# Second MLP's last tiles and first experts: splits of the experts' weights at fixed steps, each ordered behind routing and evictions; the seventh tile's logits later

## The chip, the core and the metric

The kernel runs on one core of a Trainium2 chip. Its time is the device time of one execution in microseconds (us): 430.04 us median of three runs (427.2 to 432.1). One further execution was profiled; it took 430.29 us, and the recorded span of its instructions is 428.2 us.

## The reference

Three layers follow each other; each needs the one before.

```python
attn = softmax(q @ k.T / 8 + decay bias, causal) @ v           # 2 batches x 8 heads, 576 positions, depth 64
x    = attn as 1152 tokens x 512
h    = x @ w_in;  x = (h * cos(h)) @ w_out                     # 512 -> 2048 -> 512, "the MLP"
logits = x @ w_gate;  expert = argmax(logits)                  # 8 experts, top 1
disp[expert, position of the token within the expert] = x      # capacity 288 per expert
y   = relu(disp[e] @ w1[e]) @ w2[e]                            # 512 -> 1024 -> 512, for each expert
out[token] = softmax weight * y[expert, position]
```

## The kernel before

Every float32 operand is held as two float16 parts (high and low), and each product is three float16 products.

**MLP, second product.** 1152 tokens are nine tiles of 128 (T = 0 to 8). `l2_wide` does tiles 0 to 4 side by side, `l2r` does tiles 5 to 8 one after the other, each in 8 steps of two of the 16 slices of the inner dimension: six matmuls a step (line 867). At a tile's end `l2_end` evicts the sum: for tiles 7 and 8 a float32 copy into `xq` (L856, ACT), and for all tiles the row's high part (L858, ACT) and low part (L859, DVE).

**Routing**, woven into the same steps by `l2r`: `route_a` turns the tile, by a DMA transpose on SP's queue for tiles 0 to 6 (L895), by TensorE and a copy on ACT for tiles 7 and 8 (L900, L902). `route_b`, RD = 2 steps later, makes the logits (L917, or L914 in float32), their maximum and the one-hot row on DVE (L927 to L931), the position within the expert by a matmul with a triangle (L936), the count `cnt` (L946), and a scatter of the row into `disp` in HBM (L947, POOL). After tiles 4 and 7 `partial` chooses, from the counts so far, which expert is worked on second and third; its number is loaded into a register of SP (L1170). Before tile 7's routing `hook` issues the DMA transposes `eX<-disp` of the first 144 rows of the first two experts (L1013) and their meta rows (L1020). After tile 8 `counts` orders the experts, SP loads seven numbers (L1210, L1211), issues `eX<-disp` for the rows of these two experts that came later (80 rows each in the shape that ran), and loads the shape number `fl` (L1342), on which every engine branches into its arm.

**Experts' weights.** An expert's w1 and w2 come as eight pieces of 128x1024 float32 (512 KB): SP loads a piece into a staging buffer `ws` (L969 for w1, L973 for w2; three buffers until the first experts, then four), `split` makes the high part on ACT (L658) and the low part on DVE (L659), and the buffer is free again. `e_weights` is a generator: each `next` first fills the free buffers, then splits one piece. The first expert's eight pieces are split beside `l2_wide`. The second's eight and four of the third's come from `ahead`, one per step from step 10 on wherever the expert's number is known; the third's last four follow after `counts`. The remaining 40 pieces are loaded and split in the arm.

**First experts**, `expert`: eight groups of 12 matmuls (L1044) give the hidden layer, each evicted by ACT (L1046) and DVE (L1047) into `eH`; then four groups of 24 matmuls d0 to d3 (L1066), each copied by ACT into `xq` (L1068); then eight transposes (L1073), and the result is scaled (L1052) and scattered into `out` (L1053). RF = 2 groups of the first expert run before tile 8's routing ends, and LA = 4 groups of the second before the first's d0.

**What sets the order.** A scheduler orders each engine's instructions at build time from the program's order and its own estimate; at run time every engine takes its instructions strictly in that order. `after(keys, ...)` adds an edge of order behind the last instruction stored under a key of `gate`; in the kernel before a split stands behind the last `ev` (eviction of an expert) and `cnt` (end of `counts`).

Of the kernel before, what the change touches and what calls it, by code (L numbers as in the profile page):

```python
# [15 lines left out]
ALU = mybir.AluOpType  # L16
# [9 lines left out]
W3P = 12  # L26
# [26 lines left out]
RP = 2  # L53
RD = 2
RF = 2
W2P = 24
# [21 lines left out]
def kernel(ctx, tc, q, k, v, s, w_in, w_out, wg, w1, w2, out, cap, wide):  # L78
# [773 lines left out]
    def l2_end(T, xp):  # L852
        r = work.tile([128, ROW], I32, tag="row", name="row", bufs=6)
        xf = xq[:, 0:DM] if T >= NDT else None
        if T >= NDT:
            nc.scalar.activation(xf, xp, AF.Copy, scale=2.0 ** -2)  # L856
        rh = r[:, 0:DM].bitcast(F16)
        nc.scalar.activation(rh[:, 0:DM], xp, AF.Copy, scale=2.0 ** -8)  # L858
        nc.vector.scalar_tensor_tensor(rh[:, DM:2 * DM], xp, 2.0 ** -8, rh[:, 0:DM], ALU.mult, ALU.subtract)  # L859
        nc.gpsimd.tensor_copy(r[:, DM + 1:ROW], tokid[:, T:T + 1])  # L860
        rows[T] = (r, xf)
# [29 lines left out]
    def route_a(T):  # L891
        r, xf = rows[T]
        if T < NDT:
            xr = work.tile([128, 2 * KD, 128], F16, tag="xr", name="xr", bufs=2)
            nc.sync.dma_start_transpose(out=xr, in_=r[:, 0:DM].bitcast(F16))  # L895
            rows[T] = (r, xr)
        else:
            tp = bank("pt")
            for kk in range(KD):
                nc.tensor.transpose(tp[:, kk * 128:(kk + 1) * 128], xf[:, kk * 128:(kk + 1) * 128], idf)  # L900
            xt = xq[:, DM:2 * DM].rearrange("p (k t) -> p k t", k=KD)
            nc.scalar.copy(xt.rearrange("p k t -> p (k t)"), tp)  # L902
            rows[T] = (r, xt)

    def route_b(T):
# [30 lines left out]
        nc.tensor.matmul(ppv, lhsT=tri, rhs=oh.to_broadcast([128, 2, E]), start=False, stop=True)  # L936
        nc.scalar.activation(ex, lp, AF.Exp, bias=m[:, 1:2], scale=LS, accum_out=m[:, 3:4])
        V.tensor_scalar(t1, ppv[:, 1, :], float(cap), float(NOTOK), ALU.is_ge, ALU.mult)
# [6 lines left out]
        V.tensor_scalar(r[:, DM:DM + 1].bitcast(F32), m[:, 3:4], 2.0 ** -17, None, ALU.mult)  # L945
        V.tensor_tensor(cnt[:, 0, :], cnt[:, 0, :], oh[:, 0, :], ALU.add)  # L946
        sc = nc.gpsimd.indirect_dma_start(  # L947
# [10 lines left out]

    def e_weights(plan, lo=0, hi=None):
        n = KD + KE // 2  # L960
# [17 lines left out]
        def fill(n):  # L978
            while todo and len(pend) < n and not (callable(todo[0][1]) and todo[0][1]() is None):
                ld(*todo.pop(0))  # L980

        fill(len(ws) - 1)
        yield
        for e, src, i in items:
# [5 lines left out]
            if i < KD:  # L990
                after("ev cnt", split, a[0][:, i, 0, :], a[0][:, i, 1, :], t, 64.0)
            else:
                j = (i - KD) * 2
                after("ev cnt", split, a[1][:, j:j + 2, 0, :], a[1][:, j:j + 2, 1, :], t.rearrange("p (a d) -> p a d", a=2), 64.0)
            yield
# [34 lines left out]
    def expert(e, ns, group, got=None):  # L1030
# [7 lines left out]
        for f in range(KE):  # L1038
# [7 lines left out]
            gate["ev"] = nc.scalar.activation(Hh[:, 0, f, :], hp[:, 0:ns], AF.Relu)  # L1046
            nc.vector.scalar_tensor_tensor(Hh[:, 1, f, :], hp[:, 0:ns], 0.0, Hh[:, 0, f, :], ALU.max, ALU.subtract)  # L1047
            yield
# [60 lines left out]
    def l2r(tiles, hook):  # L1109
# [13 lines left out]
        for T in tiles:  # L1123
            for j in range(KF // 2):
                next(gen)
                if mid and step - mid[0][1] >= RD:
                    finish()
# [29 lines left out]
    def partial():  # L1157
# [10 lines left out]
        V.tensor_copy(si, so[:, 0:1])  # L1168
        V.tensor_scalar(si, si, E - 1, E - 1, ALU.bitwise_and, ALU.bitwise_xor)
        P["o"].append(nc.values_load(si, engines=SP, min_val=0, max_val=E - 1))  # L1170
# [43 lines left out]
    def experts(plan, group):  # L1214
# [25 lines left out]

        gate.pop("ev", None)
        gate.pop("cnt", None)

# [53 lines left out]
    with ExitStack():  # L1297
        if True:
# [3 lines left out]
            items = KD + KE // 2  # L1302
            pre = e_weights([(i, i if i < NF else (lambda i=i: P["o"][i] if i < len(P["o"]) else None)) for i in range(NK)])
            run((l2_wide(range(WN), seq(wo, take(pre, items + 1)), L2F), KF + 1))
# [10 lines left out]
            def ahead(steps):  # L1315
                k = items
                for i in range(steps):
                    if i > KF // 2 + 1 and k < min(len(P["o"]) * items, 2 * items + KD):
                        next(pre)
                        k += 1  # L1320
                    yield
                while k < 2 * items:
                    next(pre)
                    k += 1

# [4 lines left out]
            phase, phase1 = (expert(h, HEAD, "out0", ex_.pop(h)) for h in range(NH))  # L1330
            for _ in range(RF):
                next(phase)
            next(tail)
            regs = counts()
            for _ in range(KE // 2):
                next(pre)
            order, first = registers(*regs)
            for h in range(NH):
                n = max(p[h] for p in PROFILES)
                e_rows(h, n, at(P["o"][h], first[h], n))  # L1340
            run((seq(take(phase, KE - RF), take(phase1, LA), phase, phase1), 2 * (KE + KD)), (take(pre, items), W3P))
            level = nc.values_load(regs[0], min_val=0, max_val=len(LIMITS))  # L1342
# [42 lines left out]
```

## Time and profile before

| | |
|---|---|
| median of three runs | 430.04 us |
| profiled execution | 430.29 us, span 428.2 us |
| TensorE (PE) | 395.1 us busy, 92% |
| VectorE (DVE) / ScalarE (ACT) / GpSimd (POOL) | 311.8 / 274.8 / 149.2 us busy |
| loads of the experts' weights | 64 of 512 KB, on SP's queue |

The second product of the MLP runs from about 194 to 293 us, the first two experts' 144 rows from 293 to 325 us, the arm from there to the end. A row of a timeline gives the start and the length of an instruction or a run of like ones; in brackets stands how long the engine was idle before it, and what ended that. SPq is SP's instruction queue: its rows give when a DMA was issued, not when it landed.

### The profile page before, as it was taken

Reading aid. Unit: us, or ns where it says so; the run is one execution under the profiler, and the core shown is the slowest. Engines: PE = TensorE matmul, PEld = TensorE weight load, DVE = VectorE, ACT = ScalarE, POOL = GpSimd, SP = SyncE. Lnnn points to the kernel's source line nnn. Section 1 sums busy time; section 2 is a strip of 40 time slices with the busy share of each in tenths; the row PEclk is TensorE's granted clock in tenths of the full one; section 3 lists DMA queues with packets and bytes.
Section 4 is the critical chain, followed back from the end, with each engine's and each line's share of the span. In section 5 each row is a group of like instructions: output and inputs, shape, how many; then the busy total and the mean of one; then the engine's idle time right before and its main releaser. Section 6 shows DMA issues by size and latency. Waiting matters only on the chain.

```text
span 428.2 us, 10640 instructions
## 1 busy us (share of the span) xinstructions
PE 395.1 (92%) x3928; PEld 281.6 (66%) x3928; DVE 311.8 (73%) x768; ACT 274.8 (64%) x630; POOL 149.2 (35%) x261
## 2 busy tenths in 40 slices
PE   2799999999999999999999999797998999999783
PEld 2588888886666666654444454354997999987552
DVE  7769999749999599989885664672842477877670
ACT  6679989986878677775234532533734477777560
POOL 7668887563554445455000032010011011122100
PEclk9989999999999999999999999899999999999998
DMA  7979795203369932323667456947759298998851
GB/s 166 210 173 190 165 203 151 72 2 100 98 188 328 369 124 92 88 70 98 183 204 230 116 128 206 280 110 222 252 148 216 61 314 264 308 330 265 264 209 30
DMA packets 90003, 77.38 MB, mean 181 GB/s; under 512 B 62768, under 2 KB 70960, under 8 KB 89942
## 3 DMA queue, kind: packets, MB, share of 16 engines
q1 hardware_dynamic: 86934, 71.62, 59.5%
q0 software_dynamic: 1952, 4.73, 3.2%
q8 instruction: 33, 0.54, 0.5%
q10 hardware_dynamic: 1056, 0.26, 0.3%
q14 instruction: 28, 0.23, 0.2%
HBM read 57.66 MB, written 12.28 MB: 163 GB/s over the span
## 4 chain that ended last, share of the span: by engine, by line
PE 32%; DMA 9%; DVE 7%; issue 5%; ACT 4%; SPq 2%; POOL 1%; POOLq 0%; ACTq 0%; DVEq 0%
DMA ws<-in_moe_w_dram 8%; PE ps_mm L867 7%; PE ps_sm L867 5%; PE ps_pt L1044 3%; PE ps_s L1066 3%; PE ps_mm L1044 2%; PE ps_s L867 2%; PE ps_pt L867 2%; PE ps_s L1044 2%; PE ps_pt L1066 2%; PE ps_mm L1066 2%; DVE gall L659 1%; ACT gall L658 1%; DVE y L818 1%; SPq L1013 1%
## 5 line engine op out<-in xcount | busy, mean ns | idle before, releaser
L812 PEld LDWEIGHTS <-win 128*128 128x128 f16 x576 | 56.3, 98 | 37.0
L867 PEld LDWEIGHTS <-gall 128*128 128x128 f16 x432 | 41.3, 98 | 49.3 <-issue 2.5
L867 PE MATMUL ps_mm<-wout,gall 128*128 128x512 f16 x240 | 57.9, 387 | 0.3 <-DVE n__2954 L826 0.3
L659 DVE SCALAR_TENSOR_TENSOR gall<-ws,gall 128x1024 f16<-128x1024 f32 x32 | 38.8, 1221 | 23.2 <-ACT gall L658 22.1
L1053 POOL DMA_INDIRECT out_dram<-gall,eM x15 | 18.8, 1252 | 98.4 <-ACT gall L1052 77.4
L658 ACT ACTIVATE gall<-ws 128x1024 f16<-128x1024 f32 x32 | 33.7, 1056 | 26.8 <-DMA ws<-in_moe_w_dram 26.8
L658 ACT ACTIVATE wout<-ws 128x512 f16<-128x512 f32 (+1 forms) x32 | 27.3, 860 | 23.7 <-DVE ws L681 18.5
L241 ACT ACTIVATE z<-z,st 128x256 f32<-128x256 f32 (+4 forms) x72 | 41.9, 586 | 0.7 <-DVE st L241 0.7
L947 POOL DMA_INDIRECT disp<-row,rsli x9 | 9.2, 1017 | 94.0 <-ACT rm L928 48.5
L241 DVE CUSTOM_DVE_ANT_0 z<-ps_s,zm 128x512 f32<-128x512 f32 (+3 forms) x72 | 34.5, 511 | 10.0 <-PE ps_s L244 8.8
L659 DVE SCALAR_TENSOR_TENSOR wout<-ws,wout 128x512 f16<-128x512 f32 (+1 forms) x32 | 30.4, 955 | 8.2 <-ACT wout L658 8.0
L812 PE MATMUL ps_s<-xT,win 128*128 128x384 f16 x192 | 34.2, 326 | 0.0
L812 PE MATMUL ps_pt<-xT,win 128*128 128x384 f16 x192 | 33.8, 326 | 0.0
L812 PE MATMUL ps_mm<-xT,win 128*128 128x384 f16 x192 | 33.8, 326 | 0.0
L247 PE MATMUL ps_pt<-idf,z 128*128 128x128 f32 x192 | 30.2, 282 | 1.3 <-DVE p L241 1.3
L1044 PEld LDWEIGHTS <-gall 128*128 128x128 f16 x480 | 27.0, 97 | 3.7 <-issue 1.9
L825 ACT ACTIVATE y<-y,quarter 128x384 f32<-128x384 f32 x48 | 29.2, 609 | 0.1
L241 ACT COPY p<-ps_pt 128x512 f32<-128x512 f32 (+2 forms) x48 | 25.2, 525 | 5.9 <-PE ps_pt L247 5.5
L659 DVE SCALAR_TENSOR_TENSOR win<-ws,win 128x1024 f16<-128x1024 f32 x16 | 19.4, 1225 | 11.7 <-ACT win L658 11.7
L247 PEld LDWEIGHTS ps_pt<-idf,z 128*128 128x128 f32 x192 | 23.1, 144 | 6.3 <-issue 1.5
L244 PE MATMUL ps_s<-kT,qT 128*128 128x384 f16 (+7 forms) x128 | 23.9, 307 | 1.1 <-DMA kT<-bt 0.6
L658 ACT ACTIVATE win<-ws 128x1024 f16<-128x1024 f32 x16 | 16.8, 1055 | 10.9 <-DMA ws<-in_moe_w_dram 10.9
(495 smaller groups left out, 891.9 us busy)
## 6 DMA issues: line engine op xcount, KB each, us to landing
ws<-in_moe_w_dram SPq DMA_DIRECT2D x64, 512.0 KB
ws<-in_moe_w_in_dram SPq DMA_DIRECT2D x16, 512.0 KB
ws<-in_moe_w_out_dram SPq DMA_DIRECT2D x16, 512.0 KB
disp<-zc SPq DMA_DIRECT2D x18, 257.0 KB
out_dram<-zc SPq DMA_DIRECT2D x9, 256.0 KB
qf<-in_q_dram SPq DMA_DIRECT2D x16, 128.0 KB
vf<-in_v_dram SPq DMA_DIRECT2D x16, 128.0 KB
kf<-in_k_dram SPq DMA_DIRECT2D x14, 128.0 KB
```

The costliest lines, as they stand in the source:

```text
L241: return pin(f(*a, **kw))
L244: return pin(nc.tensor.matmul(out_, **kw))
L247: return pin(nc.tensor.transpose(out_, in_, id_))
L658: nc.scalar.activation(hi, src, AF.Copy, scale=sc)
L659: (eng or nc.vector).scalar_tensor_tensor(lo, src, sc, hi, ALU.mult, ALU.subtract)
L812: nc.tensor.matmul(hp[:, 0:CH], lhsT=win[a][:, kk, fs], rhs=xT[:, x_, kk, xs], start=(n == 0), stop=(n == 3 * KD - 1))
L825: nc.scalar.activation(y, y, AF.Sin, scale=TWO_PI, bias=quarter)
L867: gate["pe"] = nc.tensor.matmul(xp, lhsT=G[c][:, a, f, ts], rhs=wout[w_][:, f, :], start=(f == 0 and n == 0), stop=(f == KF - 1 and n == 2))
L947: sc = nc.gpsimd.indirect_dma_start(out=disp, out_offset=bass.IndirectOffsetOnAxis(ap=sli.bitcast(U32), axis=0), in_=r, in_offset=None, bo ...
L1044: gate["pe"] = nc.tensor.matmul(hp[:, 0:ns], lhsT=a1[:, kk, a, fs], rhs=X[:, x_ * KD + kk, 0:ns], start=(n == 0), stop=(n == 3 * KD - 1))
L1053: sc = nc.gpsimd.indirect_dma_start(out=out, out_offset=bass.IndirectOffsetOnAxis(ap=M[:, b, 1:2].bitcast(U32), axis=0), in_=y, in_offset= ...
L1066: nc.tensor.matmul(yp[:, 0:ns], lhsT=a2[:, f, w_, d * 128:(d + 1) * 128], rhs=Hh[:, a, f, :], start=(n == 0), stop=(n == 3 * KE - 1))
```

## The change

The splits before the arm are made at fixed steps, two tables say where: `AHEAD` for the second expert's eight pieces (steps of tiles 5 to 8; step 16 is the first of tile 7), `HEADS` for the third's eight (groups of the first experts; negative ones are the two that run ahead, 0 is after `counts`). Every split now also stands behind the last eviction or routing instruction on its engine (`act`, `dve`). After each split the freed buffer's load is asked for at once (`ctl["fill"]`). The logits of tile 6, the seventh, come RL = 5 steps after its turn instead of 2.

```diff
+RL = 5
+AHEAD = (16, 17, 18, 20, 22, 24, 26, 28)
+HEADS = (-2, -1, 0, 0, 3, 5, 7, 9)
...
-        nc.scalar.activation(rh[:, 0:DM], xp, AF.Copy, scale=2.0 ** -8)
-        nc.vector.scalar_tensor_tensor(rh[:, DM:2 * DM], xp, 2.0 ** -8, rh[:, 0:DM], ALU.mult, ALU.subtract)
+        gate["act"] = nc.scalar.activation(rh[:, 0:DM], xp, AF.Copy, scale=2.0 ** -8)
+        gate["dve"] = nc.vector.scalar_tensor_tensor(rh[:, DM:2 * DM], xp, 2.0 ** -8, rh[:, 0:DM], ALU.mult, ALU.subtract)
...
-            nc.scalar.copy(xt.rearrange("p k t -> p (k t)"), tp)
+            gate["act"] = nc.scalar.copy(xt.rearrange("p k t -> p (k t)"), tp)
...
-        nc.scalar.activation(ex, lp, AF.Exp, bias=m[:, 1:2], scale=LS, accum_out=m[:, 3:4])
+        gate["act"] = nc.scalar.activation(ex, lp, AF.Exp, bias=m[:, 1:2], scale=LS, accum_out=m[:, 3:4])
...
-        V.tensor_tensor(cnt[:, 0, :], cnt[:, 0, :], oh[:, 0, :], ALU.add)
+        gate["dve"] = V.tensor_tensor(cnt[:, 0, :], cnt[:, 0, :], oh[:, 0, :], ALU.add)
...
+        if ctl is not None:
+            ctl["fill"] = lambda: fill(len(ws))
...
-                after("ev cnt", split, a[0][:, i, 0, :], a[0][:, i, 1, :], t, 64.0)
+                after("ev cnt act dve", split, a[0][:, i, 0, :], a[0][:, i, 1, :], t, 64.0)
...
-            nc.vector.scalar_tensor_tensor(Hh[:, 1, f, :], hp[:, 0:ns], 0.0, Hh[:, 0, f, :], ALU.max, ALU.subtract)
+            gate["dve"] = nc.vector.scalar_tensor_tensor(Hh[:, 1, f, :], hp[:, 0:ns], 0.0, Hh[:, 0, f, :], ALU.max, ALU.subtract)
...
-                if mid and step - mid[0][1] >= RD:
+                if mid and step - mid[0][1] >= (RL if mid[0][0] == NDT - 1 else RD):
...
             def ahead(steps):
-                k = items
                 for i in range(steps):
-                    if i > KF // 2 + 1 and k < min(len(P["o"]) * items, 2 * items + KD):
+                    if i == AHEAD[0] - 4:
+                        ctl["fill"]()
+                    for _ in range(AHEAD.count(i)):
                         next(pre)
-                        k += 1
+                        ctl["fill"]()
                     yield
-                while k < 2 * items:
-                    next(pre)
-                    k += 1
...
-            for _ in range(RF):
+            ctl["fill"]()
+
+            def pulls(i):
+                for _ in range(HEADS.count(i)):
+                    next(pre)
+                    ctl["fill"]()
+
+            for i in range(RF):
                 next(phase)
+                pulls(i - RF)
             next(tail)
             regs = counts()
-            for _ in range(KE // 2):
-                next(pre)
+            pulls(0)
             order, first = registers(*regs)
...
-            run((seq(take(phase, KE - RF), take(phase1, LA), phase, phase1), 2 * (KE + KD)), (take(pre, items), W3P))
+            for i, _ in enumerate(seq(take(phase, KE - RF), take(phase1, LA), phase, phase1)):
+                pulls(i + 1)
```

Lines of the changed kernel stand 3 to 13 further down: its L661 is L658 of the kernel before, L859, L861 and L905 are L856, L858 and L902, L1051 is L1046, L1073 is L1068, L1217 is L1211, L1018 is L1013, L976 is L973, L1355 is L1342. In the rows of the order `ws_90`, `ws_91` and `ws_92` are the three staging buffers, `ws_4090` and `ws_4079` the fourth one, `gall` is where the second and third experts' split weights go.

First place: ACT at the end of tile 8 (`xq<-ps_mm` is its float32 copy, `xq<-ps_pt` its turned copy for the logits). Before:

```order
L658 ACTIVATE gall<-ws_90 128x1024
L856 ACTIVATE xq<-ps_mm 128x512
L858 ACTIVATE row<-ps_mm 128x512
L658 ACTIVATE gall<-ws_91 128x1024
L902 COPY xq<-ps_pt 128x512
L658 ACTIVATE gall<-ws_92 128x1024
L1046 ACTIVATE eH<-ps_s 128x144
```

With the change:

```order
L661 ACTIVATE gall<-ws_92 128x2x512
L859 ACTIVATE xq<-ps_mm 128x512
L861 ACTIVATE row<-ps_mm 128x512
L905 COPY xq<-ps_pt 128x512
L1051 ACTIVATE eH<-ps_s 128x144
L661 ACTIVATE gall<-ws_90 128x1024
```

The third expert's first three splits stood ahead of or between tile 8's evictions; now its first stands behind them and behind the first eviction of an expert. On PE the logits of tile 6 move from behind 38 of the matmuls that follow tile 5's L936 to behind 49, and its L936 follows 5 matmuls later instead of 9.

Second place: ACT at the four copies of the first expert's d0 to d3. Before:

```order
L658 ACTIVATE gall<-ws_90 128x2x512
L1068 COPY xq<-ps_s 128x144
L1068 COPY xq<-ps_pt 128x144
L1068 COPY xq<-ps_mm 128x144
L1068 COPY xq<-ps_s 128x144
L1052 ACTIVATE gall<-ps_pt,eM_3443 72x512
```

With the change:

```order
L1073 COPY xq<-ps_s 128x144
L1073 COPY xq<-ps_pt 128x144
L661 ACTIVATE gall<-ws_92 128x2x512
L1073 COPY xq<-ps_mm 128x144
L661 ACTIVATE gall<-ws_4079 128x2x512
L1073 COPY xq<-ps_s 128x144
L1057 ACTIVATE gall<-ps_pt,eM_3443 72x512
```

The third expert's last two splits, all done before d0's copy until now, stand ahead of the copies of d2 and d3.

Third place: SP's queue between the last loads of the third expert and the branch. Before, the last two of these loads come first:

```order
L973 ISA
L973 DMA ws_4090<-in_moe_w_dram 128x2x512
L973 ISA
L973 DMA ws_90<-in_moe_w_dram 128x2x512
L1210 TENSOR_LOAD si
```

With the change:

```order
L1217 TENSOR_LOAD si
L1217 ISA x2
L1018 ISA
L1018 DMA_TRANSPOSE eX<-disp 128x8x80
L1018 ISA
L1018 DMA_TRANSPOSE eX<-disp 128x8x80
L976 ISA
L976 DMA ws_92<-in_moe_w_dram 128x2x512
L976 ISA
L976 DMA ws_4079<-in_moe_w_dram 128x2x512
L1355 TENSOR_LOAD fl
```

These two loads, which the two splits of the second place read, now stand behind the seven register loads and both `eX` transposes of the later rows.

## Rows read from the trace of the kernel before

**Rows 1.** Stretches: us, busy PE, PEld, DVE, ACT, POOL, PEclk, DMA share, GB/s.
```profile
274.00:278.00 4.00, 3.87 (x21) 1.61 (x22) 2.25 (x7) 2.61 (x6) 0.00 (x0) 0.57 0.96 294
296.00:298.00 2.00, 1.32 (x19) 1.31 (x20) 1.82 (x2) 2.00 (x5) 0.00 (x0) 1.00 0.85 314
380.00:400.00 20.00, 18.11 (x224) 14.39 (x222) 12.87 (x20) 13.62 (x28) 3.16 (x2) 1.00 0.87 294
```
**Rows 2.** The chain that ended last, 255 to 345 us: start, us, what.
```profile
262.47 4.16 DMA ws<-in_moe_w_dram
273.07 1.07 ACT gall L658
282.08 3.22 DMA disp<-row,rsli
```
**Rows 3.** The timeline of PE.
```profile
263.10 6.85 PE L867 MATMUL ps_mm<-wout,gall 128*128 128x512 f16 x31
274.13 0.46 PE L917 MATMUL ps_s<-wgs,xr 128*128 128x8 f16 x12 [2.62 <-ACT gall L658]
274.45 3.77 PE L867 MATMUL ps_mm<-wout,gall 128*128 128x512 f16 x9
296.68 0.65 PE L900 MATMUL ps_pt<-idf,xq 128*128 128x128 f32 x4 [2.95 <-ACT xq L856]
303.74 0.17 PE L1181 MATMUL ps_sm<-cnt,onesm 128*128 128x8 f16 x1
306.81 1.66 PE L1066 MATMUL ps_s<-eH,win 128*128 128x144 f16 x24
313.48 0.49 PE L1073 MATMUL ps_mm<-idf,xq 128*72 128x128 f32 x3
313.81 0.91 PE L1044 MATMUL ps_s<-eX,gall 128*128 128x144 f16 x12
```
**Rows 4.** The timeline of ACT.
```profile
267.61 0.58 ACT L858 ACTIVATE row<-ps_mm 128x512 f16<-128x512 f32 x1
295.09 1.06 ACT L658 ACTIVATE gall<-ws 128x1024 f16<-128x1024 f32 x1 [7.80 <-DMA ws<-in_moe_w_dram]
313.01 0.28 ACT L1068 COPY xq<-ps_s 128x144 f32<-128x144 f32 x1 [1.22 <-PE ps_s L1066]
345.86 1.06 ACT L658 ACTIVATE wout<-ws 128x1024 f16<-128x1024 f32 x1 [0.16 <-DMA ws<-in_moe_w_dram]
```
**Rows 5.** The timeline of DVE.
```profile
275.30 0.16 DVE L927 TENSOR_REDUCE rm<-ps_s 128x1 f32<-128x8 f32 x1
275.95 0.23 DVE L931 TENSOR_SCALAR roh<-rw,rm 128x8 f16<-128x8 f32 x1
304.67 0.16 DVE L1192 TENSOR_SCALAR si<-si 1x8 int32<-1x8 int32 x1
```
**Rows 6.** The timeline of SP's queue.
```profile
269.59 1.27 SPq L895 DMA_TRANSPOSE xr<-row  x1
291.45 6.31 SPq L969 DMA_DIRECT2D ws<-in_moe_w_dram  x4
310.64 2.77 SPq L1013 DMA_TRANSPOSE eX<-disp  x2
340.71 4.62 SPq L973 DMA_DIRECT2D ws<-in_moe_w_dram  x3
```
**Rows 7.** The timeline of POOL.
```profile
305.44 0.97 POOL L947 DMA_INDIRECT disp<-row,rsli  x1 [11.89 <-DVE ky L1198]
```
**Rows 8.** Two lines' instructions, 240 to 332 us: duration in ns, first and last start.
```profile
L1210 SPq TENSOR_LOAD <-si x5: 172/272/488, 304.9 to 307.2; - x5
L1211 SPq TENSOR_LOAD <-si x2: 275/276/276, 308.0 to 308.9; - x2
```

More of the change, by code (lines that the diff above doesn't have):

```diff
@@ L957, with e_weights @@
     wb = []
-    def e_weights(plan, lo=0, hi=None):
+    def e_weights(plan, lo=0, hi=None, ctl=None):
         n = KD + KE // 2
@@ L990, in e_weights @@
             if i < KD:
-                after("ev cnt", split, a[0][:, i, 0, :], a[0][:, i, 1, :], t, 64.0)
+                after("ev cnt act dve", split, a[0][:, i, 0, :], a[0][:, i, 1, :], t, 64.0)
             else:
                 j = (i - KD) * 2
-                after("ev cnt", split, a[1][:, j:j + 2, 0, :], a[1][:, j:j + 2, 1, :], t.rearrange("p (a d) -> p a d", a=2), 64.0)
+                after("ev cnt act dve", split, a[1][:, j:j + 2, 0, :], a[1][:, j:j + 2, 1, :], t.rearrange("p (a d) -> p a d", a=2), 64.0)
             yield
@@ L1168, in partial @@
         V.tensor_copy(si, so[:, 0:1])
-        V.tensor_scalar(si, si, E - 1, E - 1, ALU.bitwise_and, ALU.bitwise_xor)
+        si_ = V.tensor_scalar(si, si, E - 1, E - 1, ALU.bitwise_and, ALU.bitwise_xor)
+        gate["dve"] = si_
         P["o"].append(nc.values_load(si, engines=SP, min_val=0, max_val=E - 1))
@@ L1239, in pull @@
                 state["fed"] += 1
-        gate.pop("ev", None)
-        gate.pop("cnt", None)
+        for key in ("ev", "cnt", "act", "dve"):
+            gate.pop(key, None)
         def adv(e, k):
@@ L1302 @@
             items = KD + KE // 2
-            pre = e_weights([(i, i if i < NF else (lambda i=i: P["o"][i] if i < len(P["o"]) else None)) for i in range(NK)])
+            ctl = {}
+            pre = e_weights([(i, i if i < NF else (lambda i=i: P["o"][i] if i < len(P["o"]) else None)) for i in range(NK)], 0, None, ctl)
             run((l2_wide(range(WN), seq(wo, take(pre, items + 1)), L2F), KF + 1))
```

## Prediction

> **What bounds the kernel now.** I read the stretches first: PE is busy nearly all the time, and late in the arm the DMA engines are too (294 GB/s, and 18.1 us of PE in the 20 us from 380) [rows 1]. So there PE and the loads of the weights run as one loop: a piece is loaded, split, its buffer freed and loaded again, and the splits stand in order behind PE's evictions. The first loads of the arm that need a freed buffer go out at 340.71 [rows 6], on such a split. A shift of PE at the arm's start is therefore a shift of the end; loads that merely arrive early are not. Then I read the chain and PE's timeline over the stretch that the change touches, 263 to 325 us. The reader is to see two waits of PE there, both behind a split.
>
> Wait A: PE stands 2.62 us ahead of tile 6's logits at 274.13 [rows 3], since that tile's turn was issued at 269.59 only [rows 6]; its eviction L858 had come at 267.61, behind a split [rows 4]. The chain names the split that ended on ACT at 274.14 [rows 2] as the releaser, but the logits don't read it; I take the DMA of the turn. Wait B: PE stands 2.95 us ahead of tile 8's transposes at 296.68, released by the copy L856 [rows 3]; on ACT that copy came behind the split at 295.09, which had waited for its load [rows 4], and SP could issue that load at 291.45 only [rows 6].
>
> After wait A the next nine matmuls took 3.77 us, 0.419 each, against 0.221 for the 31 from 263.10 [rows 3]; the granted clock was 0.57 in that stretch, mostly the lower level of 1.2 GHz, and 1.00 right after wait B [rows 1]. So one long wait cost 9 x 0.198 = 1.8 us more and a slightly longer one cost nothing more.
>
> **The change, part by part.**
>
> *Tile 6's logits later.* 49 matmuls stand ahead of them, counted from tile 5's L936 at 263.10: 263.1 + 49 x 0.221 = 273.9. Tile 6's eviction no longer stands behind a split, so its turn is issued up to 2 us before 269.59; from issue to use it took 4.5 us (269.59 to 274.13) [rows 3, 6]: there by 272 to 273. Wait A and its slow matmuls go: 2.62 + 1.8 = 4.4. But on DVE the maximum L927 still stands behind the same four splits, and the fourth waits for a load that goes out only when the first has freed its buffer; ACT had that split at 273.07 [rows 2], and nothing here brings it forward. So L927 stays at 275.3 and the one-hot row L931 is done at 276.2 [rows 5]. L936 is due 5 matmuls after the logits, at 273.9 + 0.3 + 1.1 = 275.3: a new wait of 0.9 us (bounds: 0, and the 2.6 of the old one). Net 3.5. Tile 6's scatter goes out about 4 us earlier than 282.08, since its index chain on DVE is no longer cut by splits; with it go the first `eX` transposes, the third expert's number and the loads of 291.45, to about 287.6.
>
> *Second expert's splits at fixed steps.* The same eight splits; ACT and DVE have room there, and PE waits for none of them. Nothing.
>
> *Third expert's first splits behind tile 8's evictions.* Wait B goes, 2.95. PE pays 0.1 (10 instead of 12 matmuls cover the copy), and on DVE two splits now stand ahead of tile 8's one-hot row, the second waiting for its load: 0.6 us at L936 and the counts (bounds: 0; and 2, if that load comes a split late). Net 2.25.
>
> Sum so far 5.7 us. The order also puts the counts L1181 behind 80 matmuls of the experts instead of 96, 16 x 0.064 = 1.0 us (48 of them lie between 303.74 and 306.81 [rows 3]), of which PE itself gains nothing. So the counts come at 303.74 - 6.7 = 297.0, and d0 starts at 301.1 instead of 306.81. That would be the gain if nothing came after.
>
> *The third expert's last two pieces.* Here I think the gain ends. Their splits stand on ACT ahead of the copies of d2 and d3, and their loads stand on SP behind seven register loads and two `eX` transposes. From rows: L1192, whose result the first register load reads, ended 1.1 us after the counts (304.83) [rows 3, 5]; so now at 298.1. The seven loads took from 304.9 to 309.4, 4.5 us [rows 8]: 302.7. The transposes also need tile 8's scatter, which would go out at 305.44 - 6.7 = 298.7 and lands after 3.2 us, as tile 6's did [rows 2], or at most 5.2, as 305.44 to 310.64 bounds it [rows 6, 7]: 301.9 to 303.9. The two take 2.77 us to issue [rows 6]: 305.5 to 306.7. A load after such a pause can be split 3.6 us (291.45 to 295.09) or 4.2 us (262.47) after its issue [rows 2, 4, 6]: 309.1 to 310.9. Then ACT needs a split (1.06), d2's copy (0.28), the second split (1.06) and d3's copy (0.28) [rows 4], PE the last transposes (0.49) [rows 3], 3.2 in all: the second expert's next group starts at 312.3 to 314.1, against 313.81 before [rows 3]. Without the wait it would have been 308.1. So PE waits 4.2 to 6 us there, and of the 5.7 us between -1.5 and +0.3 are left; I take the middle, -0.6. DVE's two low parts follow ACT's within 1.3 us, before the evictions of that group are due.
>
> *Clock.* The new wait is longer than A and B, so a stretch at 1.2 GHz behind it is likely but not sure: price 0 (as after B) to 1.8 us (as after A) [rows 1, 3]. I take 0.6, since only one of the two old waits shows it and a part of the matmuls there lies beside ACT's two scaling copies. The Trainium skill (TensorE: Matmul & The Clock Gate, "What's actually happening") says that an array left idle falls back to half clock and that activity releases it: wait A agrees, wait B does not, and by the page the sum would be 1.2 us later.
>
> *Loads of the arm.* Its first loads go out some 6 us earlier, but their splits stand behind PE's evictions in the arm: no gain. The order of the first two splits on DVE changes, so that the second w2 load of that expert leaves about 1.5 us behind the first at 340.71 instead of at once: nothing, at most 0.5, since both still come before the third, whose split has not moved.
>
> Sum: -0.6 + 0.6 = 0. The profiled execution took 430.29 us, 0.25 above the median of the runs shown; so against the median 430.0.
>
> **Rivals.**
>
> 1. *Forecast, the gain turns into a wait at d2 and d3:* 428.5 to 432 us. For it: on ACT and SP what stands behind a waiting instruction waits too, as wait B shows, and the chain from the counts to the load is made of measured rows.
> 2. *The gain comes through:* the loads would have to land by 304 us, or the arm be set by when its first loads begin and not by PE. Then 5.7 us, less up to 1: 424.3 to 425.3. Against it: even if the scatter cost nothing, register loads and transposes put the load's arrival past 309. For it: the register loads took 0.64 us each from one to the next though one lasts 0.17 to 0.49 [rows 8], so part of that time may be gone; half of the gain would give 427.
> 3. *Slower, by one mechanism:* the late load lands later still. Tile 8's scatter takes its 5.2 us, and the load the 5.1 us that 340.71 to the split at 345.86 took [rows 4, 6]: it lands at 311.8, and the next group starts at 315.0, 1.2 us later than before; behind a wait of 7 us all 48 matmuls of four groups run at 1.2 GHz, 48 x 0.064 = 3.1 more: 434.3. It decides when the load lands after 311. Against it: little else is on the DMA queues then.
> 4. *The change doesn't do what it says:* wait A has the cause that the chain names, and stays. Then the counts and all behind them come 3.5 us later than summed: 433.
>
> Chances: 0.56, 0.21, 0.14, 0.09. About 1% (4.3 us) is what a measurement of this kernel can tell from no change. Faster by over 1% is below 425.7: rival 2 without its half way, 0.17, and 0.02 of the forecast's own tail, 0.19. Slower by over 1% is above 434.3: half of rival 3 and a little of rival 4, 0.10. Within 1%: 0.71. The range leaves out a part of rival 2 and half of rival 3: 424.8 to 433.6.
>
> **What would show it.** In the profile of the changed kernel: no idle time ahead of L917 and L900 where 2.62 and 2.95 stood; one of about 1 us ahead of tile 6's L936; d0 near 301; ACT idle for a DMA of `ws` between the copies of d1 and d2; PE idle 4 to 6 us ahead of the transposes L1073, perhaps with a granted clock below 1 behind it; the arm starting within 1 us of before. The prediction is wrong if the two late loads are issued before 303 us, or if the second expert's next group starts before 311.

## The result and the profile after

The changed kernel took 432.68 us (median of 22 runs, 430.21 to 438.12) beside 430.22 us for the kernel before in the same session; the ratio is 1.0084, 95% interval 1.0064 to 1.0103. Two more sessions gave 1.0063 (1.0031 to 1.0096) and 1.0053 (1.0017 to 1.0089). The ratios leave out the executions in the chip's slower state; the quotients of the medians of all executions are 1.0057, 1.0080 and 1.0034. The forecast was no change, 430.0 us. By the ratios the change is slower by 0.5 to 0.8 per cent, 2.3 to 3.6 us; by the medians it is 1.5 to 3.5 us. That is inside the range stated, 424.8 to 433.6 us, but it is a change.

The profiled execution took 432.67 us, its span 430.6. Line numbers are 3 to 13 higher than before: L939 is the one-hot matmul that was L936, L1071 the d matmuls (L1066), L1078 the transposes (L1073), L661 and L662 the two halves of a split (L658, L659). Tile 5's one-hot matmul stands at 265.05 here and at 263.07 in the profile of before; the profiles e5 and e12 below show that the kernel before can stand as late. All times of the two kernels are therefore compared **after tile 5's one-hot matmul**; to set a row of after beside one of before, take off 1.98.

The timeline of PE in the changed kernel (start, us, engine, line, operation, count, then the idle time before it and what released it):
```profile
265.08 10.73 PE L870 MATMUL ps_mm<-wout,gall 128*128 128x512 f16 x49
275.65 0.45 PE L920 MATMUL ps_s<-wgs,xr 128*128 128x8 f16 x12
...
278.33 0.17 PE L939 MATMUL ps_sm<-roh,tri 128*128 128x16 f16 x1 [1.08 <-DVE roh L934]
...
292.44 0.66 PE L903 MATMUL ps_pt<-idf,xq 128*128 128x128 f32 x4
...
298.50 0.17 PE L939 MATMUL ps_sm<-roh,tri 128*128 128x16 f16 x1 [0.60 <-DVE rm L946]
...
299.05 0.17 PE L1187 MATMUL ps_sm<-cnt,onesm 128*128 128x8 f16 x1
...
301.95 0.91 PE L1049 MATMUL ps_s<-eX,gall 128*128 128x144 f16 x12 [0.94 <-DVE eH L1052]
...
304.20 1.66 PE L1071 MATMUL ps_s<-eH,win 128*128 128x144 f16 x24
...
313.85 0.30 PE L1078 MATMUL ps_pt<-idf,xq 128*72 128x128 f32 x1 [3.27 <-ACT xq L1073]
...
315.31 0.37 PE L1078 MATMUL ps_pt<-idf,xq 128*72 128x128 f32 x1 [1.06 <-ACT xq L1073]
...
316.12 1.65 PE L1049 MATMUL ps_s<-eX,gall 128*128 128x144 f16 x12
317.56 1.53 PE L1049 MATMUL ps_pt<-eX,gall 128*128 128x144 f16 x12
318.93 0.91 PE L1049 MATMUL ps_mm<-eX,gall 128*128 128x144 f16 x12
...
328.45 0.53 PE L1049 MATMUL ps_pt<-eX,win 128*128 128x64 f16 x12 [0.81 <-ACT gall L1057]
```
Waits A and B [rows 3] are gone: nothing stands before L920 and L903. In their place are 1.08 us at tile 6's one-hot matmul, 0.60 at tile 8's, 0.94 at the second expert's second group, and 4.33 us at the transposes of d0 to d3. The counts and d0, which came at 303.74 and 306.81 [rows 3], are 6.7 and 4.6 us sooner after tile 5 (299.05 and 304.20, less 1.98). The second expert's next group, 313.81 before [rows 3], is 0.33 us later (316.12 less 1.98), and its first 24 matmuls run mostly at half speed: 1.65 and 1.53 us where 0.91 is full.

ACT at the place of the long wait:
```profile
307.40 0.28 ACT L1073 COPY xq<-ps_pt 128x144 f32<-128x144 f32 x1 [0.76 <-PE ps_pt L1071]
312.57 1.06 ACT L661 ACTIVATE gall<-ws 128x1024 f16<-128x1024 f32 x1 [4.90 <-DMA ws<-in_moe_w_dram]
313.53 0.26 ACT L1073 COPY xq<-ps_mm 128x144 f32<-128x144 f32 x1
314.04 1.06 ACT L661 ACTIVATE gall<-ws 128x1024 f16<-128x1024 f32 x1 [0.24 <-DMA ws<-in_moe_w_dram]
315.00 0.26 ACT L1073 COPY xq<-ps_s 128x144 f32<-128x144 f32 x1
```
The reader is to see the copy of d1, then 4.90 us in which ACT waits for the load of a split, and the copies of d2 and d3 each behind such a split. SP's queue, and then the chain of waits, show where that load was:
```profile
305.61 2.60 SPq L1018 DMA_TRANSPOSE eX<-disp  x2
308.81 1.22 SPq L976 DMA_DIRECT2D ws<-in_moe_w_dram  x2
```
```profile
309.65 4.36 DMA ws<-in_moe_w_dram
```
Both late loads go out behind the register loads and the two transposes; the second one is the link of the chain ahead of ACT's split at 314.04, 4.36 us on its way. The transposes in turn waited 1.1 us for the scatter of tile 8's rows into `disp`. This chain comes to the loads from four splits on DVE, but that of e1 (the changed kernel again) from the scatter, 4.93 us on its way, and the transposes; e6 below bears e1 out. The granted clock by stretch (us, busy PE, PEld, DVE, ACT, POOL, PEclk, DMA share, GB/s):
```profile
274.00:278.00 4.00, 3.25 (x28) 1.55 (x27) 1.68 (x4) 1.35 (x3) 0.00 (x0) 1.00 0.81 298
296.00:298.00 2.00, 1.90 (x31) 1.77 (x29) 1.95 (x3) 1.56 (x5) 0.00 (x0) 1.00 0.95 379
314.00:318.00 4.00, 2.94 (x22) 2.56 (x21) 2.11 (x2) 2.75 (x5) 0.98 (x2) 0.68 0.94 367
```
The 0.57 of the first stretch [rows 1] has become 1.00; the half clock has moved to 314 to 318.

### The profile page after: what moved, and what is told of

It is laid out like the page before. It is cut to its first block, busy times and chain, and to the rows that moved or that the text cites. A ratio compares the mean times of both kernels' runs of the same rounds, so it can differ in the third digit from the quotient of the medians.

```text
span 430.6 us, 10643 instructions
## 1 busy us (share of the span) xinstructions
PE 395.8 (92%) x3928; PEld 283.6 (66%) x3928; DVE 313.0 (73%) x768; ACT 274.8 (64%) x630; POOL 149.9 (35%) x261
## 4 chain that ended last, share of the span: by engine, by line
PE 67%; DMA 13%; DVE 6%; ACT 5%; issue 4%; SPq 2%; POOL 1%; ACTq 0%; POOLq 0%; DVEq 0%
DMA ws<-in_moe_w_dram 10%; PE ps_s L815 7%; PE ps_mm L815 7%; PE ps_pt L815 7%; PE ps_mm L870 7%; PE ps_pt L250 5%; PE ps_sm L870 5%; PE ps_s L247 4%; PE ps_mm L247 4%; DVE gall L662 3%; PE ps_s L870 2%; PE ps_pt L870 2%; PE ps_pt L1071 2%; PE ps_pt L1049 2%; PE ps_s L1071 2%
## 5 line engine op out<-in xcount | busy, mean ns | idle before, releaser
L870 PEld LDWEIGHTS <-gall 128*128 128x128 f16 x432 | 41.0, 97 | 49.2 <-issue 1.4
L870 PE MATMUL ps_mm<-wout,gall 128*128 128x512 f16 x240 | 56.3, 379 | 0.0
L662 DVE SCALAR_TENSOR_TENSOR gall<-ws,gall 128x1024 f16<-128x1024 f32 x32 | 38.8, 1221 | 17.9 <-ACT gall L661 17.4
L661 ACT ACTIVATE gall<-ws 128x1024 f16<-128x1024 f32 x32 | 33.6, 1056 | 20.5 <-DMA ws<-in_moe_w_dram 20.3
L661 ACT ACTIVATE wout<-ws 128x512 f16<-128x512 f32 (+1 forms) x32 | 27.4, 864 | 25.5 <-DVE ws L684 18.8
L662 DVE SCALAR_TENSOR_TENSOR wout<-ws,wout 128x512 f16<-128x512 f32 (+1 forms) x32 | 30.4, 955 | 7.7 <-ACT wout L661 7.6
L1049 PEld LDWEIGHTS <-gall 128*128 128x128 f16 x480 | 28.4, 100 | 3.6 <-DVE gall L662 1.7
L662 DVE SCALAR_TENSOR_TENSOR win<-ws,win 128x1024 f16<-128x1024 f32 x16 | 19.5, 1225 | 12.7 <-ACT win L661 12.7
L661 ACT ACTIVATE win<-ws 128x1024 f16<-128x1024 f32 x16 | 16.8, 1054 | 12.3 <-DMA ws<-in_moe_w_dram 12.3
```

Source lines behind the costliest of these rows:

```text
L661: nc.scalar.activation(hi, src, AF.Copy, scale=sc)
L662: (eng or nc.vector).scalar_tensor_tensor(lo, src, sc, hi, ALU.mult, ALU.subtract)
L870: gate["pe"] = nc.tensor.matmul(xp, lhsT=G[c][:, a, f, ts], rhs=wout[w_][:, f, :], start=(f == 0 and n == 0), stop=(f == KF - 1 and n == 2))
L1049: gate["pe"] = nc.tensor.matmul(hp[:, 0:ns], lhsT=a1[:, kk, a, fs], rhs=X[:, x_ * KD + kk, 0:ns], start=(n == 0), stop=(n == 3 * KD - 1))
```

## The experiments

Theory (L): the change wins its time up to d0, and the two late loads, by way of ACT's order, take it back with a half-clock stretch on top. Rivals: the loss lies ahead of the change (U); the arm behind the branch takes back whatever is won (A); the later logits cost it (R). The other letters are explained in the expectations in which they stand.

One table serves all. The places are us after tile 5's one-hot matmul, from each run's profiled execution; "tile 5" is that matmul's own time, the last column the ratio to the kernel before in the same session.

| run | tile 5 | tile 6's one-hot | d0 | next group | arm | arm to end | ratio (95%) |
|---|---|---|---|---|---|---|---|
| before, first | 263.07 | 14.98 | 43.74 | 50.74 | 61.93 | 103.2 | |
| e5, before | 266.10 | 14.95 | 46.81 | 53.81 | 65.18 | 102.4 | |
| e12, before | 265.41 | 14.88 | 44.38 | 51.38 | 62.56 | 103.7 | |
| changed, first | 265.05 | 13.28 | 39.15 | 51.07 | 63.40 | 102.2 | 1.0084 (1.0064-1.0103) |
| e1, changed | 264.40 | 13.42 | 39.67 | 51.82 | 64.24 | 103.0 | 1.0063 (1.0031-1.0096) |
| e9, changed | 264.92 | 13.55 | 39.85 | 51.75 | 63.92 | 103.6 | 1.0053 (1.0017-1.0089) |
| e2, splits late | 265.39 | 13.76 | 39.94 | 46.94 | 59.81 | 103.6 | 0.9956 (0.9922-0.9991) |
| e3, third expert as before | 264.11 | 13.72 | 43.94 | 50.94 | 62.03 | 103.6 | 1.0038 (1.0012-1.0064) |
| e4, logits two steps | 264.51 | 9.70 | 38.05 | 50.12 | 62.01 | 105.6 | 1.0045 (1.0008-1.0081) |
| e6, loads first | 265.98 | 13.71 | 39.66 | 50.06 | 62.14 | 104.7 | 0.9985 (0.9953-1.0016) |
| e10, loads first | 266.42 | 13.41 | 39.94 | 49.33 | 60.66 | 105.3 | 0.9971 (0.9933-1.0008) |
| e7, late and two steps | 269.12 | 10.06 | 38.40 | 45.40 | 58.11 | 101.6 | 0.9895 (0.9851-0.9939) |
| e8, after last group | 265.92 | 10.05 | 38.39 | 45.39 | 56.64 | 104.6 | 0.9846 (0.9787-0.9905) |
| e11, after last group | 264.63 | 9.92 | 38.25 | 45.25 | 56.42 | 107.1 | 0.9889 (0.9831-0.9946) |

e1 to e4 shared one session, e5 to e8 another, e9 to e12 a third; the kernel before had medians of 431.7, 434.7 and 433.7 us in them, so times of different sessions are not subtracted.

**e1 and e9: the changed kernel again (no edit).**

> The changed kernel once more, to separate what belongs to it from what belonged to one execution. Its first profile was already 1.98 us behind the kernel before at tile 5's one-hot matmul (265.05 against 263.07 us), with a 2.60 us wait in the attention stage that the profile of before lacks, although the instructions up to there stand in the same order. Theory L (the late loads: two loads at 308.81 us, behind the register loads and two transposes, keep two splits and with them the copies of d2 and d3 waiting): the wait in the attention stage is one execution's own; in the new profile either it is gone or the d2 and d3 copies still come about 4 to 5 us after d1's, and the time is again 431.5 to 434. Rival U (the loss sits upstream of the change): the 2 us before tile 5 are there again and the distance from tile 5's one-hot matmul to the end is within 1 us of the 165.1 us of before.

> The changed kernel a third time, beside the altered queue and the best version, because the kernel before measured 431.7 us on the chip of the first four runs and 434.7 on that of the next four, so that ratios from different chips may not be subtracted. Theory L: its ratio to the kernel before is again above 1.00 (1.004 to 1.010), unless the kernel before itself loses its clock more often here. Rival C (the kernel before has a clock loss of its own behind its second wait that comes on some chips only, and the verdict changes sign with it): 0.995 to 1.002.

Both came out slower than before again, at 435.19 us each; e1's time is above the 431.5 to 434 that theory L named, in a session in which the kernel before had 431.7. The waits at d2 and d3 are there every time: 3.53 and 0.73 us in e1, 3.30 and 0.94 in e9. Rival U's condition did not hold: the 2.60 us wait in the attention stage is in neither profile. Rival C did not hold either: e9's ratio is 1.0053.

**e5 and e12: the kernel before again (no edit).**

> The kernel before once more, for a second profile of it. In its first profile tile 5's one-hot matmul stood at 263.07 us, in five profiles of the changed kernel and its relatives at 264.1 to 265.4, with the same instructions ahead of it. Theory L: 263.07 was an early execution, and here it lies between 263.5 and 265.5, with 61 to 63 us from there to the arm's first matmul. Rival U (something ahead of tile 5 is slower in the changed kernel): again at 263.1 or below.

> A third profile of the kernel before. In its first one TensorE's wait of 2.95 us for tile 8's row left the granted clock at 1.00 in 296 to 298 us, in the second a wait of 3.20 us at the same place was followed by 0.50 in 302 to 308 us, and the arm came 3.3 us later after tile 5's one-hot matmul. Theory C: the wait for tile 8's row leaves half clock behind in some executions, so 62 or 65 us from tile 5's one-hot matmul to the arm, with nothing between. Rival N (the second profile was disturbed in more than this place): about 62.

Tile 5 stands at 266.10 and 265.41: the 263.07 of the first profile was an early execution, and the changed kernel's three (264.40 to 265.05) lie within the kernel before's own three. Rival U falls, though e5 missed both numbers of theory L: tile 5 came later than 265.5, and the arm 65.18 us behind it and not 61 to 63. PE's timeline in e5, and the stretch behind its second wait:
```profile
277.14 0.46 PE L917 MATMUL ps_s<-wgs,xr 128*128 128x8 f16 x12 [2.60 <-DMA xr<-row]
...
299.93 0.66 PE L900 MATMUL ps_pt<-idf,xq 128*128 128x128 f32 x4 [3.20 <-ACT xq L856]
```
```profile
302.00:308.00 6.00, 6.00 (x47) 6.00 (x46) 3.86 (x11) 3.30 (x9) 0.00 (x0) 0.50 0.69 206
```
and the same in e12:
```profile
276.60 0.46 PE L917 MATMUL ps_s<-wgs,xr 128*128 128x8 f16 x12 [2.75 <-DMA xr<-row]
...
299.14 0.66 PE L900 MATMUL ps_pt<-idf,xq 128*128 128x128 f32 x4 [2.92 <-ACT xq L856]
```
```profile
300.00:306.00 6.00, 5.47 (x82) 5.20 (x80) 4.88 (x12) 4.53 (x13) 0.00 (x0) 1.00 0.78 208
```
Two things are to be seen. The releaser of wait A is here named as the turned row, `xr`, as the prediction had taken it against the chain of the first profile. And wait B left the clock full after 2.95 [rows 3] and 2.92 us, but half after 3.20, so that e5's arm came 2.6 to 3.3 us later than in the other two: theory C's lateness was there once in three profiles. Rival N is not seen between tile 5 and the arm: e5's wait B ends 33.83 us after tile 5, beside 33.61 and 33.73, and from d0 to the arm it takes 18.37 us, beside 18.19 and 18.18.

**e2: the last two splits behind the copies.**
```diff
-HEADS = (-2, -1, 0, 0, 3, 5, 7, 9)
+HEADS = (-2, -1, 0, 0, 3, 5, 16, 18)
```


> The changed kernel with its last two splits pulled after steps 16 and 18 in place of 7 and 9, so that they stand on ACT and DVE behind the copies of d2 and d3, the two outputs and one more group of the second expert; SP's order is the same. Theory L: ACT's waits of 4.90 and 0.24 us ahead of d2 and d3's copies no longer reach TensorE, whose waits of 3.27 and 1.06 us and the half-clock stretch behind them (about 1.3 us) vanish: 427 to 428.5 us, 4 to 5.5 below the changed kernel and 1.5 to 3 below the one before. Rival A (the arm behind the branch takes it back, because its own loads and the third expert's last pieces set its start): d0 to d3 run without a wait but the end moves by less than 1 us, 431.5 to 433. Rival U (the loss is upstream): 431 to 433 too, with 2 us missing before tile 5.

429.52 us, 0.9956 of before, and 5.7 us or 1.3 per cent below e1's 435.19 in the same session. PE and ACT of e2:
```profile
312.33 0.91 PE L1049 MATMUL ps_s<-eX,gall 128*128 128x144 f16 x12
...
317.68 0.28 PE L1071 MATMUL ps_pt<-eH,gall 128*128 128x144 f16 x2 [0.56 <-ACT eH L1051]
...
318.97 0.22 PE L1071 MATMUL ps_pt<-eH,gall 128*128 128x144 f16 x1 [0.70 <-DVE eH L1052]
```
```profile
311.53 0.28 ACT L1073 COPY xq<-ps_s 128x144 f32<-128x144 f32 x1 [1.22 <-PE ps_s L1071]
...
313.77 1.06 ACT L661 ACTIVATE gall<-ws 128x1024 f16<-128x1024 f32 x1
```
d3's copy now waits for PE alone, and the split finds its load there. d0 came 39.94 us after tile 5, as in the changed kernel; the next group followed 7.00 us later instead of 11.90 to 12.15, at full clock. Rival A did not come. Of theory L, the drop against the changed kernel is as large as named, the absolute time 1 us above it, in a session in which the kernel before was 1.5 us slower than in the first. The splits' new place costs 0.56 and 0.70 us, since evictions now stand behind them.

**e3: the third expert's splits by the old feed, the rest changed.** The edit does not bring back the order of before: there four of the eight splits came around tile 8 and the last four behind the counts; here all eight come behind the counts, four in a row and four more between the groups.
```diff
             for i in range(RF):
                 next(phase)
-                pulls(i - RF)
...
-            pulls(0)
+            for _ in range(KE // 2):
+                next(pre)
...
-            for i, _ in enumerate(seq(take(phase, KE - RF), take(phase1, LA), phase, phase1)):
-                pulls(i + 1)
+            run((seq(take(phase, KE - RF), take(phase1, LA), phase, phase1), 2 * (KE + KD)), (take(pre, items), W3P))
```


> The changed kernel, but with the third expert's eight splits fed as in the kernel before (four behind the counts, the rest by the old feed); tiles 5 to 8 and the later logits stay as changed. Theory L: waits A and B stay removed (d0 about 4 to 6 us after-tile-5 earlier than before), the last split stands ahead of d0's copy as before and its load is again the last of SP's chain, so that the second expert's next group comes within 1.5 us of where it does in the kernel before and the time is 429 to 431.5. Rival H (the new places of the third expert's splits around tile 8 and the counts are harmless, and the loss is elsewhere): 432 to 434, as the changed kernel. Rival U: 432 to 433.

433.41 us, 1.0038 of before: above theory L's band and inside rival H's. Theory L was wrong on d0, too, which was to come 4 to 6 us sooner than before and came at 43.94 after tile 5, beside 43.74. PE shows where it stayed:
```profile
303.41 0.94 PE L1049 MATMUL ps_mm<-eX,gall 128*128 128x144 f16 x12 [4.22 <-DVE eH L1052]
304.16 1.63 PE L1049 MATMUL ps_s<-eX,gall 128*128 128x144 f16 x12
```
and ACT what stood ahead of it:
```profile
295.24 1.99 ACT L661 ACTIVATE gall<-ws 128x1024 f16<-128x1024 f32 x2
298.82 1.06 ACT L661 ACTIVATE gall<-ws 128x1024 f16<-128x1024 f32 x1 [1.59 <-DMA ws<-in_moe_w_dram]
300.22 1.06 ACT L661 ACTIVATE gall<-ws 128x1024 f16<-128x1024 f32 x1 [0.34 <-DMA ws<-in_moe_w_dram]
301.18 0.27 ACT L1051 ACTIVATE eH<-ps_mm 128x144 f16<-128x144 f32 x1
```
The counts come 2.5 to 3.5 us sooner than in the changed kernel (31.6 us after tile 5), but now four splits in a row stand ahead of the first expert's next evictions on ACT, and PE waits 4.22 us there, with half clock behind it. The gain up to the counts is lost sooner, by the same mechanism: splits whose loads are late stand ahead of evictions. With either feed some splits stand in the wrong place. So e3 does not test the third expert's old places by themselves.

**e4: tile 6's logits after two steps.**
```diff
-RL = 5
+RL = 2
```


> The changed kernel with tile 6's logits two steps after its row, as before (RL = 2); the splits keep their table, and two of them then fall behind tile 6's routing on ACT and DVE. Theory L: the later logits are worth at most 1.5 us here, the wait moves into the logits, and the late loads still set the second expert's next group: 432 to 434. Rival R (the later logits make the loss, since tile 6's one-hot and everything behind it comes later by eighteen matmuls): the 1.08 us wait at tile 6's one-hot is gone and the time is 430 to 431.5.

433.60 us, 1.0045, beside 1.0063 of e1. PE:
```profile
272.77 0.46 PE L920 MATMUL ps_s<-wgs,xr 128*128 128x8 f16 x12 [1.38 <-DMA xr<-row]
...
302.56 1.66 PE L1071 MATMUL ps_s<-eH,win 128*128 128x144 f16 x24
...
312.44 0.30 PE L1078 MATMUL ps_pt<-idf,xq 128*72 128x128 f32 x1 [3.50 <-ACT xq L1073]
...
313.77 0.43 PE L1078 MATMUL ps_pt<-idf,xq 128*72 128x128 f32 x1 [0.92 <-ACT xq L1073]
```
A wait of 1.38 us for the turned row takes the place of the 1.08 at the one-hot matmul, yet d0 comes 1.1 to 1.8 us sooner after tile 5. So the later logits gain nothing here, and without them wait A is still halved: no split stands ahead of the row's eviction any more, and the turn is issued 4.38 us after tile 5 (268.89 - 264.51) instead of 6.52 [rows 6]. The late loads remain, 3.50 and 0.92 us at d2 and d3, and the next group comes 1.0 to 1.7 us sooner than in the changed kernel. The profile thus speaks for a part of rival R, against what theory L said of the later logits; its time of 430 to 431.5 did not come, 433.60 lies where theory L put it, and the intervals of e4 and e1 overlap. What e4 gained by the arm's start is not seen at the end: its arm took 105.6 us.

**e6 and e10: the late loads ahead of the register loads on SP.**
```diff
-                nc.sync.dma_start(t, s1)
+                gate["ld"] = nc.sync.dma_start(t, s1)
...
-            order, first = registers(*regs)
+            order, first = after("ld", registers, *regs)
```
(and the same mark on the load of a second-layer piece; the load of the branch's number moved ahead with them)

> The changed kernel with SP's order alone altered: the two late loads and the load of the branch's number stand ahead of the seven register loads and the two transposes. Theory L (the late loads are late because of SP's queue): they issue as soon as DVE's splits free their tiles, at about 305 and 306 us in place of 308.81, the splits on ACT run from about 309, the copies of d2 and d3 wait 3 us less, and the time falls by 2 to 4 us against the changed kernel, to 430 to 432. Rival D (their tiles come free only when DVE has done its run of four splits, at about 308.4): the loads issue at 308 or later and the time is within 1 us of the changed kernel. Rival Q (the register loads, now 4 us later, hold the transposes for the arm and the branch): the wait at d2 goes but the arm's first matmul does not come earlier, 433 to 435.

> The queue altered as in e6 (the two late loads ahead of the register loads and the transposes), beside the changed kernel on one chip. Theory L: 0.3 to 0.8 per cent below the changed kernel, 1.3 to 3.4 us, as the first copies of d2 and d3 came 1.0 to 1.8 us sooner after tile 5's one-hot matmul in e6's profile. Rival Q (nothing gained, the difference of e6 was the chip's): within 0.2 per cent of the changed kernel.

0.9985 and 0.9971 of before; beside the changed kernel in one session, 431.81 against 435.19 us, 0.8 per cent. Nothing but SP's order differs. SP and ACT of e6:
```profile
306.66 1.50 SPq L976 DMA_DIRECT2D ws<-in_moe_w_dram  x2
...
312.71 2.62 SPq L1018 DMA_TRANSPOSE eX<-disp  x2
```
```profile
310.33 1.06 ACT L661 ACTIVATE gall<-ws 128x1024 f16<-128x1024 f32 x1 [1.21 <-DMA ws<-in_moe_w_dram]
...
313.91 1.06 ACT L661 ACTIVATE gall<-ws 128x1024 f16<-128x1024 f32 x1 [2.35 <-DMA ws<-in_moe_w_dram]
```
The loads go out 3.1 us sooner after tile 5 (40.68 against 43.76), as soon as DVE's splits have freed their tiles, and the first split follows 3.2 us sooner (44.35 against 47.52). The second gains 1.1 only: its load now takes longer. Theory L holds for SP's queue, and e10 gained 3.4 us, the most that it named. e6's own time, 433.56, is not the 430 to 432 of theory L and lies in the band of rival Q, but its session had 434.73 for the kernel before, and what rival Q said did not happen: the transposes, at 312.71 in place of 305.61, did not make the arm later. Rival D's late issue did not come, though DVE's splits are now what the loads wait for. One caution: e10's next group ran at full clock behind a wait of 2.33 us and e6's did not behind 2.94, so a part of e10's gain is clock.

**e7: late splits and logits at two steps.**
```diff
-RL = 5
+RL = 2
-HEADS = (-2, -1, 0, 0, 3, 5, 7, 9)
+HEADS = (-2, -1, 0, 0, 3, 5, 16, 18)
```


> The two edits that helped, together: the last two splits pulled after steps 16 and 18, and tile 6's logits two steps after its row. With the logits at two steps alone d0 came 1.1 to 1.6 us sooner after tile 5's one-hot matmul than in the changed kernel, which the late loads then hid. Theory L: with the late splits out of the way that gain reaches the arm: 1 to 1.6 us below the 429.5 of the late splits alone, 427.5 to 428.5. Rival H (the half-clock or the second expert's own waits for evictions eat it): 429 to 430.

429.80 us beside 434.73 for before: 0.9895. The times expected were set against the session of e1 to e4, so they don't decide (429.80 would fall to rival H); the arm starts 1.7 us sooner after tile 5 than in e2, as theory L had it: up to there the two edits add up.

**e8 and e11: the last two splits behind the second expert's last group.**
```diff
-RL = 5
+RL = 2
-HEADS = (-2, -1, 0, 0, 3, 5, 7, 9)
+HEADS = (-2, -1, 0, 0, 3, 5, 19, 19)
```


> As the run with both edits, but both last splits pulled after step 19, behind the second expert's last group instead of between its groups. With steps 16 and 18 TensorE still waited 0.56 and 0.70 us at the second expert's second layer for evictions queued behind the splits on ACT and DVE. Theory L: these waits go, another 0.5 to 1.3 us: 426.5 to 428. Rival A (the splits now free two staging tiles 2 to 3 us later, and the arm's loads and first weights with them): no gain or up to 2 us worse, 428 to 430.

> The version with the last splits behind the second expert's last group and the logits at two steps, again, with more runs and beside the changed kernel. Theory L: 0.985 to 0.992 of the kernel before and 1.5 to 2.3 per cent below the changed kernel, as the arm's first matmul came 6.8 to 7.6 us sooner after tile 5's one-hot matmul than in the changed kernel's two profiles. Rival A (the arm gives it back): 0.995 or above.

429.18 us against 434.73, and 428.49 against 433.72: ratios of 0.9846 (0.9787 to 0.9905) and 0.9889 (0.9831 to 0.9946). This version beats both kernels, the changed one by 435.19 - 428.49 = 6.7 us in one session. That it beats e7 is not shown: 429.18 beside 429.80 in one session, with intervals that overlap, and 429.18 is in the band of rival A. ACT and PE of e8:
```profile
315.43 2.01 ACT L661 ACTIVATE gall<-ws 128x1024 f16<-128x1024 f32 x2
```
```profile
311.31 0.91 PE L1049 MATMUL ps_s<-eX,gall 128*128 128x144 f16 x12
...
322.56 0.53 PE L1049 MATMUL ps_pt<-eX,win 128*128 128x64 f16 x12 [0.81 <-DMA ws<-in_moe_w_dram]
```
Both splits run in one piece with their loads long there, and PE's timeline shows no wait from the counts to the arm. Rival A is seen at work but does not win: the arm starts 7 us sooner than in the changed kernel, its first matmul waits as long as there (0.81 us), but now with a load named as what ended it; it then takes 104.6 and 107.1 us to the end, 1 to 5 more than the 102.2 to 103.7 of the six profiles of the two kernels.

## Why the prediction missed

*Up to the counts it held.* The new wait at tile 6's one-hot matmul was priced 0.9 and measured 1.08; the one at tile 8's 0.6 and 0.60; the counts were summed to 297.0 and came at 299.05 - 1.98 = 297.07 (0.7 and 1.1 us later after tile 5 in e1 and e9). Wait A had the cause assumed (e5, e12), so rival 4 was wrong.

*d0 came 1.1 us later than summed:* 302.2 in place of 301.1. The sum lacked the 0.94 us at the second expert's second group, where DVE's low parts wait for ACT's evictions and these stand behind two splits with a late load. It did not matter, since the loads and not d0 set what follows.

*The mechanism held:* the gain turned into a wait at d2 and d3 for two late loads. **The failed step is the sizes of two terms of the sum: "I take the middle, -0.6" for those loads, and "I take 0.6" for the clock.** SP's two loads were to go out at 305.5 to 306.7 and did at 306.83, since the scatter ahead of the transposes took 4.93 us in e1 (priced 3.2 to 5.2) and held them 1.1 us (0.4 in e9); the first split was to start at 309.1 to 310.9 and did at 310.59, near the late bound. In e1 and e9 the loads went out at 307.5 and 307.2 on the scale of before and the first split started at 311.4 and 311.3, past both ranges. From the first split to the next group the sum had 3.2 us; it took 3.55, 3.51 and 3.50. The second split waited 0.24 us for its own load, and from the last wait of PE to the next group the transposes took 0.81 to 0.86 us instead of 0.49; the same stretch took 0.47 in e10, at full clock. So the first pair shows +0.33 us, where I had a middle of -0.6 between bounds of -1.5 and +0.3; e1 and e9 show +1.08 and +1.01 against the same profile of before, and +0.44 and +0.37 against e12.

*The clock was mis-sized too.* From the next group to the arm the changed kernel took 12.33, 12.42 and 12.17 us, the kernel before 11.19, 11.37 and 11.18: 1.1 us on average instead of 0.6, the 0.3 us of the transposes not counted, and half clock in three of three profiles. The rule of the Trainium skill that the prediction weighed (TensorE: Matmul & The Clock Gate, "What's actually happening": an idle array falls back to half clock) would have put the sum 1.2 us higher, an estimate from wait A's 1.8 us. These three profiles agree with it; waits B of 2.92 and 2.95 us left the clock full, so in this short form it does not tell which wait costs the clock.

Together: +0.33 + 1.14 = +1.47 us from tile 5 to the arm in the first pair of profiles (63.40 - 61.93), where the sum had 0; e9 and e12, of one session, show 63.92 - 62.56 = 1.36. Measured were 1.5 to 3.6 us, by session and by medians or ratios. What remains, up to 2 us, is **not settled**: ahead of tile 5 and behind the arm's start the two kernels' three profiles overlap (264.40 to 265.05 within 263.07 to 266.10, 102.2 to 103.6 beside 102.4 to 103.7). e3 and e4, which reach the arm within 0.1 us of the first profile of before, came out 0.4 per cent slower as well, so something that these profiles don't show seems to add a microsecond or two to several of the versions; no run tells it apart. One candidate, a half-clock stretch late in the arm (0.57 in 407 to 411 us of the first changed profile, 1.00 in all three profiles of before over 380 to 425), is not in e1 and e9.

Rival 3 (0.14) had the right sign and in part the right cause: its condition, a load that lands after 311, was met by the second load, which landed at 314.01 - 1.98 = 312.03. Its size was too large, as the half clock lasted for some 20 to 30 of the matmuls and not for 48. The prediction's two signs of being wrong did not come (loads at 306.83 and not before 303, the next group at 314.14 and not before 311), as both looked for a faster kernel only.

Rival 2 was right in one thing: as e8 and e11 show, a gain ahead of the arm does reach the end, 1.5 and 1.1 per cent of the time with the second edit, once nothing behind d0 waits.

## What to carry to other kernels

On an engine that takes its work in order, a piece that needs a load is placed by when its load lands, not by when its turn in a plan comes. In e8 and e11 two such pieces stood behind the evictions that PE waits for, and cost PE no wait; in the changed kernel they stood ahead of copies that PE waits for, and cost it 4.2 to 4.3 us, with a half-clock stretch in three profiles of three. Moving them turned +0.6 per cent into -0.4, and with a second edit into -1.1 to -1.5. Before 2 us are put down to a cause, profile both kernels again: three profiles of the same kernel lay 3 us apart at one place ahead of any change.

## What the runs showed of the hardware

- Waits of like length leave the clock at either level. At wait A 2.60 to 2.75 us were followed by a granted clock of 0.57 to 0.60 over the next 4 us in three profiles of three; at wait B 2.92 and 2.95 us were followed by 1.00 and 3.20 us by 0.50; at d2, 2.33 us left it full and 2.94 did not. Length alone does not tell it in these rows.
- Two loads of one size issued by SP within 1.5 us of each other were split 1.5 us apart in the changed kernel (at 312.57 and 314.04) and 3.6 us apart in e6 (310.33 and 313.91), where they went out sooner. In e6 the second took at least 313.91 - 308.16 = 5.7 us from issue to split, beside 3.7 of the first. Why was not tried.
